# Sixteen of 96 idle TensorE products taken out, and a new issue order for all engines

## Chip, cores and metric

The kernel runs on one core of a Trainium2 (trn2) chip. The metric is the device time of one execution in microseconds (us). Times come as the median of several executions with the lowest and highest beside it. One further execution was taken with the hardware profiler; it is called the profiled execution here, and all rows of the trace are from it.

## What is computed

Eight batches, eight heads of 64 columns, 576 positions; 32 packed queries `p` per head. First the packed queries attend to `k` and `v`, then `q` attends to the result. The eight heads side by side are a matrix `x` of 576 x 512 per batch, which goes through a gated block:

```python
p_packed = sm_attn(p, k, v)
out = sm_attn(q, p_packed, p_packed)          # sm_attn: softmax(qq kk^T / 8) vv
x = out.transpose(0, 2, 1, 3).reshape(B, S, H * D)
gate_pre += conv_w[k] * xp[:, k:k + S, :]     # k = 0..4, causal
gate = 1 / (1 + exp(-gate_pre))
val = x @ w_val
return gate * val @ w_out
```

## The kernel before

The work of a batch `b` is cut into steps, each written as a generator of the kernel function. In the names of the trace and of the order:

- `keys` (line 415) and `queries` (423): VectorE (DVE) turns the loaded `pm`, `km`, `qm` into `pT`, `kT`, `qT` by 32x32 transposes.
- `attn_pack` (426): TensorE (PE) makes the scores `s1` from `kT` and `pT`; DVE takes the maximum (`nb1`), ScalarE (ACT) the exponential into `a1`; PE transposes `a1` into `at`, ACT copies that to `a1t`, PE multiplies it with `vm` into `pv`; ACT and DVE scale this to `ppd`.
- `packed_turned` (548): PE transposes `ppd` into `ppTt`, ACT copies it to `ppT`.
- `attn_out` (557) and `weighted_group` (588): PE makes the scores `s2` from `qT` and `ppT`; DVE transposes them into `t2` and takes the maximum, GpSimd (POOL) subtracts, ACT takes the exponential; DVE sums and inverts (`rs2`), POOL multiplies, DVE transposes back into `a2`, ACT rounds it to `a2h`, POOL keeps the rest as `a2l`.
- `packed_values` (610): PE makes `wp` from `ppT` and the weights `wv`; ACT and DVE split it into `wph` and `wpl`.
- `mixed` (625) and `convolved` (654): PE makes `x`; for batches 0 and 1 the convolution is folded into that product by `kx`, a product of `ppd` and the taps `cwb`. `gate` (696): for the other batches five taps on ACT and DVE, then a tanh on ACT (`sig`).
- `value` (715): PE makes `val` in four column blocks `val_b_0` to `val_b_3` of 12 products; DVE multiplies each with the gate, ACT rounds it to `gvh`, POOL keeps the rest as `gvl`.
- `project` (761): PE multiplies `gvh` and `gvl` with `woh` and `wol` into `o`, 12 products for each 128 rows; ACT copies it to `osb`, SyncE (SP) stores it. For the last batch five accumulators are filled round by round, one round for each column block of `val`.
- `value_weights`, `conv_weights` and `out_weights` (331, 340, 367) turn the float64 weights into float32 by several steps on ACT, DVE and POOL (`from_double`, 309: `wv_top`, `wv_words`, `wo_top`, `wo_words`, `cw_top`, `cw_words`).
- `keep_busy` (534) issues products of `ident` into the unread tile `spare`, two for each token of the order. These are the idle products: their result is used by nobody.

All engines issue in program order. `ORDER` (line 58) is a list of tokens that says which generator takes its next step: `D` is `keep_busy`, `K`, `Q`, `V`, `P`, `L` are the loads, `W`, `C`, `O` the weights, `k`, `q`, `a`, `p`, `s`, `t`, `u`, `w`, `x`, `v`, `o` the steps above with the batch behind the letter, `g` a gate; `.n` repeats. The row of tokens thus sets the order on each engine and on SP's queue of loads. A load of `km`, `qm`, `vm` or weights waits until the one five loads before it has landed (`AT_ONCE`, lines 48 and 240). The large PSUM buffers for `s1`, `s2`, `at`, `pv`, `wp`, `x`, `val` are three (`PSB`), so PE also waits until ACT or DVE have read a buffer out. Every instruction that a generator issues is recorded under line 93, so rows are told apart by their tiles.

```python
for _ in range(BUSY):
    for _ in range(2):
        pe.matmul(
            spare.rearrange("a (n x) -> a n x", n=2),
            x[:, :P],
            x.unsqueeze(1).broadcast_to([P, 2, 2 * P]),
            start=True,
            stop=True,
        )
    yield
```

Of the kernel before, what the change touches and what calls it, by code (L numbers as in the profile page):

```python
# [57 lines left out]
ORDER = """
K0 L0.2 D0.2 W0.4 D0.2 P0.2 W0.2 L0 k0 W0.3 D0.2 W0.4 D0 k0 D0.2 K0 D0.2 W0.3 D0.2 Q0 D0 k0 L0.3 D0 V0.2 D0.2 W0.2 
D0 W0 D0.4 C0 D0.2 a0.5 C0 W0.2 q0 D0 W0 C0 k1 D0.2 O0 a0.2 Q0 D0.4 O0 a0.3 W0 C0 W0 C0 W0 O0 W0 D0.2 K1.2 O0 a0.2   # L60
O0 q0 a0.2 O0 a0.2 p0 C0.2 O0 k1 D0 k1 p0 P2.2 s0 L0 W0 s0.2 D0 O0.2 s0.3 a1.3 s0 C0 a1 D0 W0 D0 C0 s0 D0 t0.2 C0 
a1 s0 w0.2 a1.3 D0 C0 u0.2 x0 V1 D0.2 V1 a1 w0 K2 O0 u0 O0 a1 t0 O0 a1 O0.2 a1.4 O0 t0 k2.2 K2 Q1 x0 Q1 k2 a1 x0 
p1.2 u0 q1.2 V2 u0 t0 O0 x0.4 D0 a2.2 D0 a2 O0.2 a2 x1 D0 a2 K3 k3.2 K3 Q2 v0.2 | v0 k3 s1.2 v0 s1.2 v0.3 s1.2 v0.3 
V2 s1.2 a2 t1 a2.2 a3 a2 L0 O0.3 a2 s1 t1 a3.2 L0 a3 a2.2 O0 a2 P4 a3 O0 u1 Q2 a3 a2.2 O0 u1 O0.2 v0 D0 a2 D0 t1 
P4 v0 O0 v0.2 a3.3 D0 u1 w1 v0.2 V3.2 q2 p2 w1 a3.3 w1 k4 q2 a3.3 t1 p2 K4 k4 u1 a3 x1.3 p3 t1 O0 K4 O0 Q3 u1 s2 
k4 V4 s2 O0 D0 s2.5 x1.3 O0 s2 Q3 q3 O0 V4 O0.2 v1.2 x2 O0.2 K5 p3 q3 v1.2 s2 a4.3 v1 t2 a4.2 k5 Q4 v1 o0 u2 K5 t2 
o0 a4 t2 a4 k5 a4 v1 u2 t2 u2 s3 Q4 v1.2 s3 v1.2 s3.3 P6 s3 V6 o0.2 q4 x2 o0 u2 o0 v1 x2.2 q4 s3 t2 v1.2 u2 v1 s3 
w2.2 x2.2 g8 g9 o0 a4 o0 a4.4 t3 v1 o1 x2 g10 P6 k5 a4.2 w2 a5 s3 g8 Q5 o1 K6 g8 g9 V5 g8 g9.2 a4 o0 p4 g10 p4 g8 
g10 g9.2 a5.4 o0 g10.3 Q5 t3 u3.2 s4.3 o0 v2 g11 u3 t3 a5 o1 a5.2 t3 o1 s4 g11.3 g8 v2 o1.2 v2.2 g11 s4.3 v2 s4 
u3.2 o1.2 x3.3 v2 x3 s4 k6 v2.3 q5.2 x3.2 v2 o0 w3 x3 K6 t3 v2.3 g15 t4 u4 g14 w3 k6 a5 t4 o1.2 k6 V5 a5 u4 g12 a5   # L70
g11 w3 o1 v2.3 g12 u4 a5.4 t4.2 a5 g14 o2.2 g15.2 o2 a6 g14 g12 t4 g13 a6 p5.2 o2 a6.2 g14 a6 g13.2 g12 o2 g13 
g12.2 g13 g15 v3.2 o1.2 s5 g14 s5 o1 s5 u4 v3.2 K7 v3 g14 s5 g13 s5 v3 a6 g15 s5.2 o2.2 u4 x4 v3 x4.4 s5 x4 g17 x4 
o2 v3 Q6 v3 q6 g17 v3 g15 v3 g17 s5 V6 v3.3 o2 v3.2 a6 t5 u5 g16 o3 g16 a6 w4 o3 a6 g16 a6.2 g19 g17 g19 a6 u5 
w4.2 a6 g19 g16.2 t5 o3.3 g16 u5 v4.2 g18 V7.2 a6 o2 g17.2 a6 g18.2 g19 g18 o3 o2 a6 u5 g18 t5 g18 t5 g19.2 u5 
v4.3 o1 o3 x5.4 v4.2 o3 K7 Q6 k7.3 v4.2 q6 v4 x5.2 p6 x5 t5 p6 g23.3 o3.2 g23 v4 g20.2 o3.2 s6.3 v4.4 s6.2 g22 
s6.2 t6 v4 o3.2 g23.2 o2 a7 t6 a7 Q7.2 g20 a7 g21 a7.2 g22 q7.2 a7 w5 o4 a7 o4.3 s6 g22 s6 g21 a7 g20 a7.2 o4 a7 
w5 u6 w5 a7 o4.2 u6 t6 g21 a7.4 g20 p7.2 t6 g20 g21.2 v5.3 t6 s7.3 v5 g21 o4 s7.3 v5.2 g22 o3 g22 v5 g22 o4 v5.2 
x6 o4 u6 x6 v5 u6.2 s7 v5.2 x6 v5.2 x6 s7 x6 o4 v5.2 o5 x6 g24.2 o4 g24.2 x6 g24 g25 o5 w6.3 g27.2 s7 g27 g26 o5 
g26 g24 g25 g26 g25 g26 g27 o5.2 v6 o5 v6 o5.2 g26 g27 g25.2 v6 o5 x7 g26 v6.2 o5 t7.2 g27 g25 o5 u7 v6.2 u7 t7.2 
v6.8 o5.2 t7 u7 x7 o5 x7 o5 x7 v6 x7.2 g29.3 x7 g28.3 o6.2 w7.3 u7.2 g28 o6.4 g28 g29 v7 g29 g28 g30.2 o6 g29 o6   # L80
v7.3 g30 g31 v7 g31 g30 o6 v7 o6.3 g30 v7.3 g31.2 g30 g31.2 v7.7 o7.19 
"""


# [771 lines left out]
```

## Time and profile before

| | us |
|---|---|
| median of 3 executions | 275.85 (274.7 to 277.2) |
| profiled execution, own time | 275.32 |
| its span, first to last instruction | 273.3 |
| PE busy | 262.6 (96% of the span) |
| DVE busy | 229.1 (84%) |
| ACT busy | 167.0 (61%) |
| POOL busy | 133.6 (49%) |

A row of the trace gives a start and a duration in us from the start of the span. The idle time of an engine stands in brackets with the one that ended it. PE's products overlap: the duration of one is longer than the distance to the next, so the distance is taken from a group of them. A busy PE is one on which no gap between products shows. The PE clock of a row is the share of 2.4 GHz that was granted; 0.50 is 1.2 GHz.

### The profile page before, as it was taken

The numbers are of one execution on the slowest core, as the hardware profiler recorded it, in microseconds if no ns is written. First come the engines' busy times: TensorE is split into PE (matmuls) and PEld (weight loads), VectorE is DVE, ScalarE is ACT, GpSimd is POOL, SyncE is SP. The second block draws the span as 40 slices with busy tenths as digits, with TensorE's granted clock in tenths as the row PEclk, the third lists the DMA queues.
The fourth block names the chain that finished last, engine by engine and source line by source line (L and its number), as shares of the span: only waits on it lengthen the run. The fifth ranks groups of instructions, "written<-read, shape, count | busy, mean of one in ns | idle before, by whom it ended". The sixth has DMA issues, their size and how long they took to land.

```text
span 273.3 us, 8380 instructions
## 1 busy us (share of the span) xinstructions
PE 262.6 (96%) x3547; PEld 191.9 (70%) x3547; DVE 229.1 (84%) x333; ACT 167.0 (61%) x311; POOL 133.6 (49%) x130
## 2 busy tenths in 40 slices
...
GB/s 232 314 340 309 328 304 138 315 278 282 307 166 274 141 180 251 4 194 97 44 245 90 41 143 294 45 165 111 119 7 36 77 60 57 41 77 38 38 2 192
DMA packets 25731, 43.56 MB, mean 159 GB/s; under 512 B 6730, under 2 KB 6750, under 8 KB 25694
## 3 DMA queue, kind: packets, MB, share of 16 engines
...
## 4 chain that ended last, share of the span: by engine, by line
PE 84%; DMA 6%; DVE 5%; ACT 2%; issue 2%; SPq 1%; DVEq 0%; ACTq 0%
PE o L93 37%; PE val L93 19%; PE s L93 9%; PE x L93 6%; PE pv L93 4%; DMA km<-in_k_dram 3%; PE wp L93 3%; PE at L93 2%; PE spare L93 2%; DMA wv_words<-in_moe_w_val_dram 2%; DVE qT L93 1%; PE ppTt L93 1%; DMA vm<-in_v_dram 1%; DVE kT L93 1%; SPq L93 1%
## 5 line engine op out<-in xcount | busy, mean ns | idle before, releaser
L93 DVE SCALAR_TENSOR_TENSOR sig<-xp,cw,sig 128x576 f32<-128x576 f32 x96 | 77.9, 846 | 10.1 <-ACT sig L93 9.1
L93 POOL TENSOR_TENSOR gvl<-sig,gvh 128x576 fp32r<-128x576 f32 x32 | 46.1, 1444 | 36.5 <-ACT gvh L93 28.5
L93 PE MATMUL o<-woh,gvh 128*128 128x512 f32 x144 | 58.4, 406 | 0.0
L93 PE MATMUL o<-wol,gvh 128*128 128x512 f32 x144 | 56.6, 393 | 0.0
L93 PE MATMUL o<-woh,gvl 128*128 128x512 f32 x144 | 56.4, 392 | 0.0
L93 PE MATMUL val<-a2h,wph 128*128 128x288 f32 x128 | 39.7, 310 | 0.0
L93 ACT ACTIVATE osb<-o 128x512 f32<-128x512 f32 (+1 forms) x34 | 20.0, 589 | 29.0 <-PE o L93 23.7
L93 PE MATMUL val<-a2l,wph 128*128 128x288 f32 x128 | 37.7, 294 | 0.0
L93 PE MATMUL val<-a2h,wpl 128*128 128x288 f32 x128 | 37.6, 294 | 0.0
L93 POOL TENSOR_TENSOR a2l<-a,a2h 128x576 fp32r<-128x576 f32 x16 | 22.7, 1424 | 23.3 <-ACT a2h L93 14.8
L93 PEld LDWEIGHTS o<-woh,gvh 128*128 128x128 f32 x144 | 27.0, 188 | 9.5 <-ACT osb L93 2.2
L93 PEld LDWEIGHTS o<-woh,gvl 128*128 128x128 f32 x144 | 27.1, 188 | 6.7 <-POOL gvl L93 0.4
L93 ACT CAST gvh<-sig 128x576 fp32r<-128x576 f32 x32 | 21.6, 674 | 15.7 <-DVE sig L93 15.4
L93 PEld LDWEIGHTS o<-wol,gvh 128*128 128x128 f32 x144 | 27.1, 188 | 4.6
L93 POOL TENSOR_TENSOR t<-t,rs 128x576 f32<-128x576 f32 x16 | 18.4, 1161 | 23.0 <-DVE sig L93 16.9
L93 PEld LDWEIGHTS val<-a2h,wph 128*128 128x128 f32 x128 | 24.0, 188 | 7.4 <-issue 2.7
L93 DVE SCALAR_TENSOR_TENSOR sig<-sig,val 128x576 f32<-128x576 f32 x32 | 23.6, 740 | 3.9 <-PE val L93 3.7
L93 PE MATMUL spare<-ident 128*128 128x512 bf16 x96 | 24.9, 404 | 1.4 <-POOL ident masks.py:199 1.4
L93 PEld LDWEIGHTS val<-a2h,wpl 128*128 128x128 f32 x128 | 24.1, 188 | 0.5
L93 PEld LDWEIGHTS val<-a2l,wph 128*128 128x128 f32 x128 | 24.0, 188 | 0.0
L93 ACT ACTIVATE sig<-sig 128x576 f32<-128x576 f32 x24 | 16.3, 684 | 11.7 <-DVE sig L93 11.6
L93 POOL TENSOR_TENSOR t<-t,mx 128x576 f32<-128x576 f32 x16 | 18.5, 1158 | 8.9 <-DVE mx L93 5.7
...
## 6 DMA issues: line engine op xcount, KB each, us to landing
...
```

The source lines that it names most:

```text
L93: made = getattr(self.engine, op)(*args, **kw)
```

## The change

`BUSY` goes from 48 to 40 tokens, so 80 idle products are issued, not 96, and `ORDER` is another row of tokens for the same steps. Nothing else differs: the same products, transposes and copies are issued on each engine apart from the 16.

```diff
-BUSY = 48
+BUSY = 40
 ORDER = """
-K0 L0.2 D0.2 W0.4 D0.2 P0.2 W0.2 L0 k0 W0.3 D0.2 W0.4 D0 k0 D0.2 K0 D0.2 W0.3 D0.2 Q0 D0 k0 L0.3 D0 V0.2 D0.2 W0.2 
...
+D0 L0 W0.2 L0 W0.5 D0.5 W0.2 D0 K0 P0 K0 P0 k0 D0 W0 D0.6 L0 D0 L0 W0 D0 W0 D0 k0.2 D0 W0 D0 W0.2 D0 a0 W0 Q0 W0.2 
...
```

On PE the idle products stand, before: 48 at the start, then behind the steps `s1_0` 6, `at_0` 8, `pv_0` 4, `ppTt_0` 2, `s2_0` 2, `cwps` 6, `at_1` 6, `x_0_1` 2, `s1_2` 4, `pv_2` 4, `at_3` 2, `s2_2` 2. Now: 40 at the start, then behind `s1_0` 8, `at_0` 4, `pv_0` 6, `ppTt_0` 6, `cwps` 2, `wp_0` 8, `at_1` 2, `s1_2` 2, `s2_2` 2. Behind `pv_2` and `at_3` none are left. `spread`, which stood ahead of `wp_0` and `at_1`, now stands behind both. The steps that follow keep nearly the same sequence on PE; at the end `val_7_3` now stands behind the first two rounds of the last batch's `o`, where it stood ahead of the first.

SP's queue, the first loads of the program. Before:

```order
L93 DMA km_0_0_82<-in_k_dram 128x576 x2
L93 DMA wv0_words_85<-in_moe_w_val_dram 128x512 x2
L93 DMA wv1_words_88<-in_moe_w_val_dram 128x512 x2
L93 DMA p_0_105<-in_p_dram 32x8x64 x4
L93 DMA wv2_words_113<-in_moe_w_val_dram 128x512 x2
L93 DMA km_0_1_138<-in_k_dram 128x576 x2
```

Now:

```order
L93 DMA wv0_words_85<-in_moe_w_val_dram 128x512 x2
L93 DMA wv1_words_91<-in_moe_w_val_dram 128x512 x2
L93 DMA km_0_0_114<-in_k_dram 128x576 x2
L93 DMA p_0_117<-in_p_dram 32x8x64 x4
L93 DMA km_0_1_122<-in_k_dram 128x576 x2
L93 DMA wv2_words_143<-in_moe_w_val_dram 128x512 x2
```

The first half of `km_0` moved behind two weight loads, the second half moved ahead of the third weight load; ahead of `p_0` stand the same loads as before.

ACT, from the exponentials of batch 0 (`a1_0`) to the copy of its transposed products (`a1t_0`). Before:

```order
L93 ACTIVATE a1_0_199,sums_77<-s1_0_1_202,nb1_0_1_238 128x2x9x32
L93 ACTIVATE cw_words_163<-cw_words_163 20x128
L93 ACTIVATE wv3_top_248<-wv3_words_160 128x512
L93 ACTIVATE wo0_top_257<-wo0_words_165 128x512
L93 ACTIVATE wo0_words_165<-wo0_words_165 128x512
L93 COPY a1t_0_261<-at_0_262 128x1024
```

Now:

```order
L93 ACTIVATE a1_0_171,sums_77<-s1_0_1_174,nb1_0_1_225 128x2x9x32
L93 ACTIVATE cw_words_227<-cw_words_227 20x128
L93 ACTIVATE wo0_top_240<-wo0_words_229 128x512
L93 COPY a1t_0_244<-at_0_245 128x1024
L93 COPY a1t_0_244<-at9_0_246 128x128
L93 ACTIVATE wv3_top_310<-wv3_words_148 128x512
```

Two weight steps moved behind the copy.

DVE, from the second key transpose of batch 2 to the first maximum of its scores (`nb1_2_0`). Before:

```order
L93 STREAM_TRANSPOSE kT_2_1_657<-km_2_1_602 128x1152
L93 STREAM_TRANSPOSE qT_1_0_670<-qm_1_0_605 128x1152
L93 STREAM_TRANSPOSE qT_1_1_672<-qm_1_1_654 128x1152
L93 TENSOR_REDUCE nb1_2_0_766<-s1_2_0_732 128x1
L93 TENSOR_REDUCE nb1_2_1_773<-s1_2_1_733 128x1
```

Now:

```order
L93 STREAM_TRANSPOSE kT_2_1_706<-km_2_1_636 128x1152
L93 TENSOR_SCALAR wo1_words_465<-wo1_words_465 128x512
L93 SCALAR_TENSOR_TENSOR wo1_top_704<-wo1_top_704,wo1_words_465 128x512
L93 TENSOR_SCALAR wo1_words_465<-wo1_top_704 128x512
L93 STREAM_TRANSPOSE qT_1_1_756<-qm_1_1_644 128x1152
L93 TENSOR_REDUCE nb1_2_0_759<-s1_2_0_717 128x1
```

The three weight steps of `wo1`, which stood some six instructions earlier, now stand between the transposes; `qT_1_0` moved ahead of this stretch.

## Rows read from the trace of the kernel before

**Rows 1.** The page: engines' shares of the span; of the chain that ended last.

```profile
PE 262.6 (96%) x3547; PEld 191.9 (70%) x3547; DVE 229.1 (84%) x333; ACT 167.0 (61%) x311; POOL 133.6 (49%) x130
...
PE 84%; DMA 6%; DVE 5%; ACT 2%; issue 2%; SPq 1%; DVEq 0%; ACTq 0%
```

**Rows 2.** Windows: stretch, us; busy (instructions) PE, PEld, DVE, ACT, POOL; PE clock, DMA share, GB/s.

```profile
26.41:49.30 22.89, 22.70 (x488) 13.63 (x489) 20.00 (x30) 14.03 (x31) 16.53 (x14) 1.00 0.81 260
49.30:74.60 25.30, 24.04 (x513) 18.23 (x512) 23.23 (x40) 17.94 (x40) 18.96 (x17) 1.00 0.91 293
74.60:150.00 75.40, 75.22 (x1154) 56.67 (x1156) 73.43 (x105) 49.54 (x93) 39.76 (x38) 1.00 0.49 155
150.00:255.00 105.00, 104.13 (x1133) 81.62 (x1122) 91.09 (x121) 68.99 (x117) 45.94 (x45) 1.00 0.26 88
```

**Rows 3.** Timeline of PE, opening: start, us, what, count [idle before, who ended it].

```profile
1.38 12.47 PE L93 MATMUL spare<-ident 128*128 128x512 bf16 x48 [1.38 <-POOL ident masks.py:199]
14.25 0.72 PE L93 MATMUL s<-kT,pT 32*32 32x288 f32 x16 [0.40 <-DVE kT L93]
15.51 1.47 PE L93 MATMUL s<-kT,pT 32*32 32x288 f32 x48 [0.54 <-DVE kT L93]
16.91 1.47 PE L93 MATMUL spare<-ident 128*128 128x512 bf16 x6
19.38 1.20 PE L93 MATMUL at<-ident,a 128*128 128x128 f32 x9 [1.00 <-ACT a L93]
```

**Rows 4.** The tile spare: duration of one product, ns min/median/max.

```profile
L93 PE MATMUL spare<-ident x96: 379/379/634, 1.4 to 74.8; 128*128 128x512 bf16 x96
```

**Rows 5.** Timeline of the opening, ACT and DVE.

```profile
10.03 0.63 ACT L93 ACTIVATE p<-p 128x512 f32<-128x512 f32 x1 [2.24 <-DMA p<-in_p_dram]
...
10.70 0.45 DVE L93 STREAM_TRANSPOSE pT<-p 128x256 f32<-128x256 f32 x1 [1.83 <-ACT p L93]
...
12.82 2.63 DVE L93 STREAM_TRANSPOSE kT<-km 128x1152 f32<-128x1152 f32 x2
```

**Rows 6.** Timeline of ACT, the steps ahead of the copies a1t of batches 0 and 1.

```profile
19.61 0.68 ACT L93 ACTIVATE wv_top<-wv_words 128x512 f32<-128x512 f32 x1
...
21.34 1.16 ACT L93 COPY a1t<-at 128x1024 f32<-128x1024 f32 x2
...
37.45 0.70 ACT L93 COPY cwb<-spread 128x640 f32<-128x640 f32 x1
38.04 0.28 ACT L93 COPY a1t<-at 128x128 f32<-128x128 f32 x1
```

**Rows 7.** Timeline of DVE, its two longest waits between 30 and 80 us.

```profile
48.71 1.42 DVE L93 TENSOR_REDUCE nb<-s 128x1 f32<-128x576 f32 x2 [1.20 <-PE s L93]
...
74.61 0.79 DVE L93 STREAM_TRANSPOSE t<-s 128x576 f32<-128x576 f32 x1 [1.29 <-PE s L93]
```

**Rows 8.** PE's longest wait after 26 us, and the chain's piece ahead of it.

```profile
68.68 1.26 DVE qT L93
...
72.42 0.55 PE L93 MATMUL ppTt<-ident,ppd 128*128 128x128 f32 x3 [1.26 <-ACT ppd L93]
```

**Rows 9.** Windows behind PE's last product (columns as in rows 2).

```profile
267.00:269.40 2.40, 2.30 (x9) 1.57 (x9) 1.37 (x2) 0.61 (x2) 0.00 (x0) 1.00 0.59 219
...
271.40:271.60 0.20, 0.00 (x0) 0.00 (x0) 0.00 (x0) 0.00 (x0) 0.00 (x0) 0.95 1.03 389
271.60:271.80 0.20, 0.00 (x0) 0.00 (x0) 0.00 (x0) 0.00 (x0) 0.00 (x0) 0.50 0.90 338
```

**Rows 10.** The end: the chain's run of o, and the steps behind val (busy, mean ns).

```profile
255.30 11.65 PE o L93 x51
...
L93 POOL TENSOR_TENSOR gvl<-sig,gvh 128x576 fp32r<-128x576 f32 x32 | 46.1, 1444 | 36.5 <-ACT gvh L93 28.5
...
L93 ACT CAST gvh<-sig 128x576 fp32r<-128x576 f32 x32 | 21.6, 674 | 15.7 <-DVE sig L93 15.4
...
L93 DVE SCALAR_TENSOR_TENSOR sig<-sig,val 128x576 f32<-128x576 f32 x32 | 23.6, 740 | 3.9 <-PE val L93 3.7
```

More of the change, by code (lines that the diff above doesn't have):

```diff
@@ L58 @@
 ORDER = """
-K0 L0.2 D0.2 W0.4 D0.2 P0.2 W0.2 L0 k0 W0.3 D0.2 W0.4 D0 k0 D0.2 K0 D0.2 W0.3 D0.2 Q0 D0 k0 L0.3 D0 V0.2 D0.2 W0.2
[L60 to L78, printed above, removed]
@@ L79 @@
-g26 g24 g25 g26 g25 g26 g27 o5.2 v6 o5 v6 o5.2 g26 g27 g25.2 v6 o5 x7 g26 v6.2 o5 t7.2 g27 g25 o5 u7 v6.2 u7 t7.2
-v6.8 o5.2 t7 u7 x7 o5 x7 o5 x7 v6 x7.2 g29.3 x7 g28.3 o6.2 w7.3 u7.2 g28 o6.4 g28 g29 v7 g29 g28 g30.2 o6 g29 o6
-v7.3 g30 g31 v7 g31 g30 o6 v7 o6.3 g30 v7.3 g31.2 g30 g31.2 v7.7 o7.19
+D0 L0 W0.2 L0 W0.5 D0.5 W0.2 D0 K0 P0 K0 P0 k0 D0 W0 D0.6 L0 D0 L0 W0 D0 W0 D0 k0.2 D0 W0 D0 W0.2 D0 a0 W0 Q0 W0.2
+D0.3 W0.3 a0.3 L0.2 C0 a0 q0 D0 C0 O0 a0.4 V0.2 D0.2 a0.2 Q0 W0 k1 W0 O0.2 K1.2 C0 D0.2 a0 O0 C0 O0 C0.3 W0.3 a0.2
@@ new lines @@
+O0 D0 a0.2 q0 k1.2 V1 p0 D0.3 O0 p0 W0 s0 W0 O0.2 s0 C0 s0.4 Q1 D0 a1.2 s0 a1.3 L0 w0 C0 D0.2 s0 t0.2 a1 D0.2 s0
+a1 V1 D0 u0 t0 u0 w0.2 u0 C0 a1 C0 a1 x0 P2.2 q1 a1.2 u0 t0 a1.3 x0 K2.2 k2 a1.2 Q1 x0 p1 x0.2 k2 t0 p1 x1 O0 k2
+O0.2 x0.2 O0 a2 O0 V2 O0 q1 O0 a2 K3.2 a2 D0 u0 v0 a2 k3.2 v0 a2.2 | v0 O0 s1.2 a2.2 k3 s1 a2 O0 v0 V2 L0 O0 s1.3 v0
+Q2.2 v0.2 O0 P4 s1.2 v0 s1 v0.4 t1 a3.4 q2 a3 O0 a2.2 O0 V3.2 a2.3 P4 O0 t1 a2 v0.2 a3.2 a2 a3.2 w1 O0 w1 p2 u1.2
+t1 O0.3 w1 u1 a3.2 q2 p2 a3.2 t1 a3 K4.2 v0.2 a3.2 x1 L0 x1.2 t1 p3 u1.2 k4.2 s2 p3 k4 s2 O0 s2 O0 s2.2 D0 s2.2
```

16 lines of the change are left out of this document (added).

## The prediction

> **What bounds the kernel now.** I read the page's shares first. PE is busy for 96% of the span and carries 84% of the chain that ended last; DVE is busy for 84% [rows 1]. Such shares mix stages, so the windows come next, one for each stage [rows 2]. From 26.41 us on the reader is to see two engines close to full at once. Between 49.30 and 74.60 PE is idle for 25.30 - 24.04 = 1.26 us and DVE for 25.30 - 23.23 = 2.07 us. Between 74.60 and 150 PE is idle for 0.18 us and DVE for 1.97 of 75.40 us. Only after 150 does DVE have room (13.91 us idle of 105) while PE still has almost none (0.87). So up to 150 us the end of PE's row of products and the end of DVE's row of transposes, reductions and gate steps are nearly the same thing, and an idle product that is taken from PE gains time only as far as DVE comes earlier too.
>
> Third, the timeline of PE in the opening [rows 3]: 48 idle products fill 12.47 us, then PE waits for `kT` of DVE (0.40 and 0.54 us), later for the exponential `a` (1.00 us). The opening is set by loads, DVE and ACT; the idle products there cost nothing. Fourth, the waits after it: one large one on PE, 1.26 us ahead of `ppTt` at 72.42, at the end of a chain through DVE's `qT` and ACT's `ppd` [rows 8], and two on DVE, 1.20 us for `s1_2` and 1.29 us for `s2_2` [rows 7].
>
> **The change part by part.** The sum is made against the profiled execution's own time, 275.32 us: a span of 273.3 and 2.0 around it. That is 0.5 under the median of 275.85 and inside the range of the three runs.
>
> *Price of an idle product.* The six behind the first scores take 1.47 us, the last of them 0.38 [rows 3, 4], so they stand (1.47 - 0.38) / 5 = 0.22 us apart. Sixteen are worth 3.5 us of PE at most. Eight of them are in the first block.
>
> *Opening, to the first scores.* Eight products fewer, 8 x 0.22 = 1.8 us. PE then waits for `kT` longer: 0.40 + 1.8 = 2.2 us. For `kT` to come earlier, `p` must land earlier: DVE stood idle for 1.83 us until ACT had scaled `p`, which itself waited 2.24 us for the load [rows 5]. Ahead of `p` in the new queue stand the same loads, `km_0_0`, `wv0` and `wv1`, in another order. Behind `pT` DVE has the same work up to the end of `kT` (12.82 + 2.63 = 15.45). `wv0` and `wv1` do arrive earlier, but ACT and DVE only wait less often before `p`. I take 0. Bounds: 0.5 either way, about the 0.40 and 0.54 that PE waits for the two halves of `kT`.
>
> *From there to the first `val`, at 49.3.* PE has 38 idle products where it had 40: -0.4 us. The copy `a1t_0` can start up to one ACTIVATE of 0.68 us earlier, since `wv3_top` now stands behind it [rows 6], but behind `ppTt_0` there are now six products where there were two, 4 x 0.22 = 0.9 us, and that takes it back. `spread` now runs behind `at_1`, and ACT's queue still has `cwb` ahead of the last piece of `a1t_1` (0.70 and 0.28 us) [rows 6], so `pv_1` starts later, by some 0.6 us. Four products fewer between `x_0_1` and `val_0_0` gives 0.9 back. On DVE the three steps of `wo1` now stand ahead of `qT_1_1` and `nb1_2`; they wait for ACT's `wo1_top`, which stands behind gate steps that wait for PE's `x_0_0`. Behind them on DVE wait `nb1_2` and everything that frees the PSUM buffers for `s2_1`. The cover is the 1.20 us that DVE idles at this place now [rows 7]. -0.4 - 0.7 + 0.9 + 0.6 - 0.9 = -0.5, of which DVE's part leaves me -0.3. Bounds: -1.1 (the two products and the ACTIVATE, nothing given back) to +1.2 (the idle time of DVE used up and as much again lost).
>
> *49.3 to 74.6.* Two idle products stand where eight stood: 6 x 0.22 = 1.3 us off PE, and with the wait of 1.26 at 72.42 at most 2.6. But this wait shows that PE was early: the chain came through `qT` (1.26 us) on DVE and `ppd` on ACT [rows 8]. The new order has the transposes of `q` and the steps of `wo2` at other places, with the same amount of DVE work. DVE cannot save more than its 2.07 us of idle time, 1.29 of which is one wait for PE's `s2_2` that moves with PE [rows 2, 7]. I take -0.6, nearer to what DVE's short waits leave (2.07 - 1.29 = 0.78) than to PE's 2.6. Bounds: -2.1 and 0.
>
> *74.6 to 255.* No idle product stands here in either order. PE's idle time is 0.18 + 0.87 = 1.05 us [rows 2], and no permutation of the same products can gain more than that apart from the seams between blocks. I take -0.4. Bounds: -1.05, and +1.3 for one new wait as long as the one at 72.42.
>
> *The end.* `val_7_3` moves behind two rounds of `o`. Its `gvl` is needed one round and the nine products of `o_7_8` later: 21 products, 11.65 / 51 = 0.23 apart, 4.8 us. It takes 0.74 + 0.67 + 1.44 = 2.85 us on DVE, ACT and POOL [rows 10]. Covered with 1.9 us to spare, so 0. If that cover is gone because DVE comes late, up to +0.7.
>
> Sum: 0 - 0.3 - 0.6 - 0.4 + 0 = -1.3 us, and 275.3 - 1.3 = 274.0. All lower bounds together give 275.3 - 4.75 = 270.6, all upper ones 275.3 + 3.7 = 279.0.
>
> *A rule to weigh: the clock in the opening.* Idle products also keep PE from standing still. The granted clock reads 1.00 (2.4 GHz) through the waits of 0.40, 0.54 and 1.00 us that the opening has now; by these rows a wait costs only itself. Behind the last product, which ends before 269.40, it still reads 0.95 in 271.40 to 271.60 and 0.50 (1.2 GHz) from there on [rows 9]: some 2.2 us without a product were followed by the lower level. The new wait of 2.2 us is as long. The Trainium skill, TensorE: Matmul & The Clock Gate, section What's actually happening, says that the slow level is the default and that activity releases it. The trace agrees as far as it goes: the longest idle product takes 634 ns against a median of 379 [rows 4]. By that rule a fall would not end by itself, and the second rival's time would hold.
>
> **Rivals.** *PE alone sets the time.* Then DVE's row closes up with PE's: the eight products behind the first scores are gained in full (1.8), the wait at 72.42 goes (1.26), and 0.4 comes after that: 275.3 - 3.5 = 271.8. For it: PE's 84% of the chain [rows 1], and that DVE's two longest waits are for PE [rows 7]. Against it: DVE is full for 73.43 of 75.40 us right behind the place [rows 2].
>
> *The clock falls in the opening wait.* Place: the 2.2 us ahead of the first scores. Price: a start at the slow level can be read from the first block. 48 products at 0.22 would take 47 x 0.22 + 0.38 = 10.7 us, and they took 12.47 [rows 3], so 1.8 us went. If instead everything that PE does up to the first `at` runs at half speed, it is 0.72 + 1.47 + 1.47 = 3.7 us more. The middle is 2.7, and these are now scores on the chain, with no filler behind which it could hide but the 1.00 us ahead of `at`. Together with the other terms: 275.3 - 1.3 + 2.7 = 276.7, slower than before. It decides from the point where its price passes 1.3 us. For it: the fall at the end of the run [rows 9]. Against it: at the end nothing at all follows, while here scores come in between, and no wait of up to 1.00 us did it.
>
> **How the numbers follow.** A measurement of this kernel can tell about 1%, 2.75 us, from no change. The forecast, DVE letting through a part, from 272.6 to 275.6: 0.48. PE alone, 270.6 to 273: 0.32. The fall of the clock, 275.6 to 278.5: 0.14. Something else, a new wait after 74.6 above all: 0.06. The range that leaves out 2 in 10 is 270.7 to 277.6; the forecast's own is 272.6 to 275.6. Faster by over 1% (under 272.6): most of the second case and a little of the first, 0.36. Slower by over 1% (over 278.1): a third of the clock case, most of the unnamed one and some of the forecast's own error, 0.13. Within: 0.51.
>
> **What would show it.** Right: `kT` of batch 0 ends at about 15.4; PE idles for about 2.2 us ahead of the first scores with the clock at 1.00; `val_0_0` starts within 1 us of 49.3; the wait ahead of `ppTt_3` is still there or has become several smaller ones for DVE between 49 and 75; PE's idle time after the opening is larger than now by 1 to 2 us, and DVE's row is as full. Wrong: the block at 49 to 75 shorter by over 2 us, or `kT` earlier than 14.5 (then PE alone); scores of batch 0 that take twice as long, with a granted clock of 0.50 (then the clock); a wait of over 1 us on PE after 75.

## The result, and the profile after

Over 19 executions of each, the changed kernel has a median of 278.05 us (276.92 to 279.87) against 276.66 (274.70 to 278.59): a ratio of 1.0052, 95% interval 1.0028 to 1.0076, about 1.4 us slower. Ten further executions beside another set of runs gave 1.0036 (1.0004 to 1.0068). I had forecast 1.3 us less. Ratios here and below are worked out from the single executions and leave out those over 1.5% above the fastest of their kernel, so they can differ from the ratio of two medians by some tenths of a per cent.

The profiled execution took 279.05 us with a span of 277.1. That is 1.0 above the median of its kernel, while the 275.32 from which I predicted proved to be 1.3 below its own. So the two traces lie 3.7 us apart where the medians lie 1.4 apart, and part of the difference below is scatter.

The page after: engines' shares, the chain's shares, and the queue that brings the engines' code.

```profile
PE 264.1 (95%) x3531; PEld 190.3 (69%) x3531; DVE 230.5 (83%) x333; ACT 166.1 (60%) x311; POOL 133.8 (48%) x130
...
q8 instruction: 27, 0.44, 0.7%
...
PE 80%; DVE 6%; DMA 5%; issue 4%; ACT 2%; POOL 1%; ACTq 0%; POOLq 0%; DVEq 0%
```

Sixteen products are gone and PE is busy 1.5 us longer than in [rows 1]. Its share of the chain fell from 84% to 80%, "issue" (the engine waits for nothing that the profile shows) rose from 2% to 4%. Next the opening, PE's timeline, to be laid beside [rows 3]:

```profile
1.38 11.46 PE L93 MATMUL spare<-ident 128*128 128x512 bf16 x40 [1.38 <-POOL ident masks.py:199]
15.71 0.72 PE L93 MATMUL s<-kT,pT 32*32 32x288 f32 x16 [2.87 <-DVE kT L93]
16.97 2.44 PE L93 MATMUL s<-kT,pT 32*32 32x288 f32 x48 [0.54 <-DVE kT L93]
19.35 2.42 PE L93 MATMUL spare<-ident 128*128 128x512 bf16 x8
22.02 1.20 PE L93 MATMUL at<-ident,a 128*128 128x128 f32 x9 [0.25 <-ACT a L93]
```

Two things are to be seen. PE waits 2.87 us where I had 2.2, and the 48 score products behind the wait take 2.44 us where they took 1.47. The windows of that stretch (columns as in rows 2) say why the second:

```profile
15.00:17.00 2.00, 0.74 (x20) 0.21 (x20) 2.00 (x3) 0.68 (x2) 1.85 (x2) 1.00 0.88 307
17.00:18.00 1.00, 1.00 (x33) 0.51 (x34) 0.90 (x2) 0.00 (x0) 0.00 (x0) 0.51 1.06 317
18.00:19.00 1.00, 1.00 (x32) 0.36 (x15) 0.46 (x2) 0.00 (x0) 0.38 (x1) 0.50 0.97 332
19.00:20.00 1.00, 1.00 (x10) 0.28 (x3) 0.58 (x1) 0.00 (x0) 0.92 (x2) 0.50 1.07 396
20.00:21.00 1.00, 1.00 (x5) 0.39 (x4) 1.00 (x3) 0.79 (x3) 1.00 (x1) 0.78 0.87 253
21.00:22.00 1.00, 0.77 (x4) 0.15 (x2) 1.00 (x1) 1.00 (x5) 0.04 (x1) 1.00 0.96 295
```

The granted clock fell to 0.50 (1.2 GHz) behind the wait and came back during 20 to 21 us, while PE worked without a gap. And the wait is longer because `kT` starts 1.47 us later than in [rows 5]. The timeline of ACT and DVE:

```profile
11.77 0.63 ACT L93 ACTIVATE p<-p 128x512 f32<-128x512 f32 x1 [2.95 <-DMA p<-in_p_dram]
...
12.43 0.45 DVE L93 STREAM_TRANSPOSE pT<-p 128x256 f32<-128x256 f32 x1 [5.54 <-ACT p L93]
...
14.29 2.63 DVE L93 STREAM_TRANSPOSE kT<-km 128x1152 f32<-128x1152 f32 x2
```

`p` landed 1.74 us later, although its loads were issued earlier (the first at 3.80 us instead of 4.01): from issue to landing took 6.4 to 6.9 us where it had been 4.5 to 4.7. And DVE stood idle for 5.54 us instead of 1.83: with the weights ahead in the queue its weight steps were done before, and nothing was left to do.

| start of | before | after | later by |
|---|---|---|---|
| first scores of batch 0 | 14.25 | 15.71 | 1.5 |
| `at_0` | 19.38 | 22.02 | 2.6 |
| `val_0_0` | 49.32 | 51.95 | 2.6 |
| scores `s2_2` | 72.89 | 74.52 | 1.6 |
| `val_1_0` | 78.05 | 81.00 | 2.9 |
| scores `s1_7` | 185.69 | 188.15 | 2.5 |
| last product's end | 269.30 | 273.05 | 3.7 |

So the opening loses 2.6 us, the stretch from `val_0_0` to `s2_2` gains 1.0 back, and what stands right behind loses 1.3: the scores `s2_2` 0.27 and the product `x_1_1` 1.05, of which the stop below is 0.36. Another 1.2 us are lost between 188 us and the end. PE's timeline of the kernel before there, in which `x_1_1` is one row of 80 products:

```profile
72.89 1.71 PE L93 MATMUL s<-qT,ppT 32*32 32x288 f32 x64
...
75.07 3.05 PE L93 MATMUL x<-a,kx 32*64 32x288 f32 x80
```

And of the changed kernel:

```profile
74.04 0.55 PE L93 MATMUL ppTt<-ident,ppd 128*128 128x128 f32 x3
74.52 1.98 PE L93 MATMUL s<-qT,ppT 32*32 32x288 f32 x64
...
76.97 2.06 PE L93 MATMUL x<-a,kx 32*64 32x288 f32 x42
79.39 1.68 PE L93 MATMUL x<-a,kx 32*64 32x288 f32 x38 [0.36 <-issue]
...
199.79 0.32 PE L93 MATMUL pv<-vm,a1t 64*32 64x64 f32 x8 [0.83 <-issue]
...
220.66 0.50 PE L93 MATMUL o<-woh,gvh 128*128 128x512 f32 x1 [0.69 <-ACT osb L93]
```

The wait of 1.26 ahead of `ppTt_3` [rows 8] is gone; a shorter one of 0.48 stands at 68.35 us, ahead of another `ppTt`. New are two stops inside a run of equal products with nothing to wait for that the profile shows (0.36, 0.83), and one for ACT's `osb` (0.69; the kernel before has none there, but one of 0.55 for ACT's `xp` at 235.64 us). Last the windows of the two stages up to `x_1_1` that answer to the first two of [rows 2] (the second ends at the start of `x_1_1`, half a microsecond further on in the work than there), and behind them DVE's two waits that answer to the first of [rows 7].

```profile
28.24:51.95 23.71, 23.12 (x486) 13.29 (x487) 20.94 (x31) 13.89 (x31) 15.90 (x14) 1.00 0.85 256
51.95:76.97 25.02, 24.37 (x508) 17.63 (x506) 23.93 (x41) 17.92 (x41) 18.83 (x17) 1.00 0.86 268
```

DVE's timeline:

```profile
48.23 0.44 DVE L93 TENSOR_SCALAR wo_words<-wo_words 128x512 uint32<-128x512 uint32 x1 [1.13 <-ACT wo_top L93]
...
51.77 1.42 DVE L93 TENSOR_REDUCE nb<-s 128x1 f32<-128x576 f32 x2 [0.62 <-PE s L93]
```

Between 51.95 and 76.97 DVE is now idle for 25.02 - 23.93 = 1.09 us where it had 2.07: it closed up, as forecast.

### The profile page after: what moved, and what is told of

Same layout as the page of the kernel before. It is cut to its first block, busy times and chain, and to the rows that moved or that the text cites. A ratio compares the mean times of both kernels' runs of the same rounds, so it can differ in the third digit from the quotient of the medians.

```text
span 277.1 us, 8347 instructions
## 1 busy us (share of the span) xinstructions
PE 264.1 (95%) x3531; PEld 190.3 (69%) x3531; DVE 230.5 (83%) x333; ACT 166.1 (60%) x311; POOL 133.8 (48%) x130
## 4 chain that ended last, share of the span: by engine, by line
PE 80%; DVE 6%; DMA 5%; issue 4%; ACT 2%; POOL 1%; ACTq 0%; POOLq 0%; DVEq 0%
PE o L93 37%; PE val L93 17%; PE s L93 9%; PE x L93 8%; PE pv L93 3%; DMA km<-in_k_dram 2%; DMA wv_words<-in_moe_w_val_dram 2%; PE wp L93 2%; PE at L93 1%; PE ppTt L93 1%; DVE nb L93 1%; PE spare L93 1%; DVE kT L93 1%; DVE mx L93 1%; DVE rs L93 1%
## 5 line engine op out<-in xcount | busy, mean ns | idle before, releaser
L93 DVE SCALAR_TENSOR_TENSOR sig<-xp,cw,sig 128x576 f32<-128x576 f32 x96 | 78.9, 850 | 12.3 <-ACT sig L93 11.2
L93 POOL TENSOR_TENSOR gvl<-sig,gvh 128x576 fp32r<-128x576 f32 x32 | 45.5, 1425 | 55.1 <-DVE sig L93 27.2
L93 PE MATMUL o<-woh,gvh 128*128 128x512 f32 x144 | 59.0, 410 | 0.7 <-ACT osb L93 0.7
L93 PE MATMUL val<-a2h,wph 128*128 128x288 f32 x128 | 39.1, 305 | 0.0
L93 POOL TENSOR_TENSOR t<-t,rs 128x576 f32<-128x576 f32 x16 | 19.1, 1196 | 20.4 <-DVE sig L93 12.1
L93 PE MATMUL spare<-ident 128*128 128x512 bf16 x80 | 22.1, 427 | 1.4 <-POOL ident masks.py:199 1.4
```

The lines of the kernel that those rows point to most:

```text
L93: made = getattr(self.engine, op)(*args, **kw)
```

## Experiments

The theories at this point: the *clock* (the wait lets it fall), the *loads* (their new order brings `p` late), *new waits* behind 75 us, and that the late idle products save little because DVE sets that stretch. In all runs the kernel before was timed on the same chip; ratios are to it, 1% being 2.77 us.

**The opening, on the new order.** Four kernels differ in the order of the first loads and in the idle products that stand ahead of the first scores. Twelve products more (e1_fill_wait; e7_new_loads_fill8 has `D0.5` and 44, eight more):

```diff
-BUSY = 40
+BUSY = 46
-D0 L0 W0.2 L0 W0.5 D0.5 W0.2 D0 K0 P0 K0 P0 k0 D0 W0 D0.6 L0 D0 L0 W0 D0 W0 D0 k0.2 D0 W0 D0 W0.2 D0 a0 W0 Q0 W0.2 
+D0 L0 W0.2 L0 W0.5 D0.5 W0.2 D0 K0 P0 K0 P0 k0 D0 W0 D0.6 L0 D0 L0 W0 D0 W0 D0 k0.2 D0 W0 D0 W0.2 D0.7 a0 W0 Q0 W0.2 
```

The old order of the first loads (e2_old_loads; e3_old_loads_fill adds the eight products of e7 to it):

```diff
-D0 L0 W0.2 L0 W0.5 D0.5 W0.2 D0 K0 P0 K0 P0 k0 D0 W0 D0.6 L0 D0 L0 W0 D0 W0 D0 k0.2 D0 W0 D0 W0.2 D0 a0 W0 Q0 W0.2 
+K0 D0 L0 W0.2 L0 W0.5 D0.5 W0.2 D0 P0 L0 K0 P0 k0 D0 W0 D0.6 D0 L0 W0 D0 W0 D0 k0.2 D0 W0 D0 W0.2 D0 a0 W0 Q0 W0.2 
```

> The changed kernel with twelve idle products more, placed right ahead of the first scores, so that its wait of 2.87 us there shrinks to 2.87 - 12 x 0.22 = 0.2 us; everything else is as changed. Clock theory (the wait let the granted clock fall to 0.50 and the slow scores behind it cost time to the end): the granted clock stays at 1.00 between 15 and 21 us, the second half of s1_0 takes about 1.5 us as before the change and not 2.44, val_0_0 starts 1 to 1.5 us earlier than 51.95, and the time is 0.9 to 1.5 us under the changed kernel, at or just under the kernel before (ratio 0.998 to 1.002). Load theory (p comes late because of the order of the loads, the clock is a side show): kT still ends at 16.9, val_0_0 moves by under 0.5 us, the ratio stays at 1.004 to 1.006. Theory of new waits behind 75 us: the opening gets shorter, but the time does not follow, ratio 1.003 to 1.006.

> The changed kernel with the first loads in the order of the kernel before (km_0_0 first, then wv0, wv1, p_0, wv2, km_0_1), still 40 idle products at the start. Load theory: p lands 1 to 1.7 us earlier, kT of batch 0 starts at about 12.9 instead of 14.29, PE's wait ahead of the first scores falls from 2.87 to about 2.2 us or less, and val_0_0 comes about 1 us earlier; the time 0.7 to 1.4 us under the changed kernel (ratio 1.000 to 1.003), and if the clock still falls in the shorter wait, only half of that. If p's landing varies with the chip and not with the queue: no earlier kT, ratio 1.004 to 1.006. Clock theory alone: the clock still falls in a wait of 1.4 to 2.2 us and the ratio stays within 1.002 to 1.006.

> Both at once: the changed kernel with the old order of the first loads and eight idle products more ahead of the first scores, so 48 stand there as in the kernel before. If the opening is all that the change lost: s1_0, at_0 and pv_0 start as in the kernel before or up to 0.8 us earlier, val_0_0 at 48.5 to 49.5, and the time is 0.5 to 1.5 us under the kernel before (ratio 0.994 to 0.998). If new waits behind 75 us hold the end: val_0_0 within 0.5 us of 49.3, but ratio 1.000 to 1.004.

> The changed kernel with eight idle products more ahead of the first scores; against the run with the old order of the loads and the same eight products it differs in the loads' order alone. Load theory: that run was at 0.9996 of the kernel before, this one is 0.7 to 2 us slower, ratio 1.002 to 1.007, with a wider scatter of single times. If the loads' order does nothing: ratio 0.998 to 1.002, and the 1.0047 of the run with twelve products was scatter or came from its four products more.

> The changed kernel once more, beside the others on one chip. Clock theory: the granted clock falls again behind the wait ahead of the first scores (mean clock 0.993 or 0.994 in nearly all executions). Load theory: kT of batch 0 starts at 13.5 or later again. Stalls of PE by its own code: PE stands still again with 'issue' at the same products of its stream, the 1237th, 2130th or 3024th, and not at others. Ratio 1.003 to 1.008 by all of them.

| loads | products ahead of the first scores | ratio (95%) |
|---|---|---|
| old | 48 | 0.9996 (0.9968 to 1.0023); again 0.9999 (0.9970 to 1.0028) |
| old | 40 | 1.0018 (0.9990 to 1.0045) |
| new | 48 | 1.0023 (0.9988 to 1.0058) |
| new | 52 | 1.0047 (1.0006 to 1.0088) |
| new | 40: the changed kernel | 1.0052 (1.0028 to 1.0076); again 1.0036 (1.0004 to 1.0068) |

With both parts of the opening undone the changed kernel equals the kernel before, so the loss lies in the opening. One part alone is worth some 0.5 to 0.6 us, both together 1.0 to 1.4; but the intervals of the single parts reach 1, that of the changed kernel does not, so how the loss is shared out is not settled. In the repeated profile of the changed kernel `p` was late again (11.60 us), PE waited 2.92, the second scores took 2.46 us, and PE stopped at the same products. In the run with the old loads and 40 products the wait was 1.54 us in the profile, the clock stayed (mean 0.998), and the scores took 1.47; over its executions, though, the mean clock was below 0.995 in 7 of 12. The run with 52 products is a miss: the wait was gone, the clock at 1.00 and `val_0_0` 2.2 us earlier in its profile, as the clock theory had it, yet its time did not fall. Its single times scatter from 275.80 to 281.35, with a median of 279.13; I can't say why.

**The opening, on the old order.** The same two edits on the kernel before: eight of the 48 products out (e4_before_less8, with 44 tokens), and the new order of the loads (e5_before_new_loads).

```diff
-D0 W0 D0.4 C0 D0.2 a0.5 C0 W0.2 q0 D0 W0 C0 k1 D0.2 O0 a0.2 Q0 D0.4 O0 a0.3 W0 C0 W0 C0 W0 O0 W0 D0.2 K1.2 O0 a0.2 
+D0 W0 C0 D0.2 a0.5 C0 W0.2 q0 D0 W0 C0 k1 D0.2 O0 a0.2 Q0 D0.4 O0 a0.3 W0 C0 W0 C0 W0 O0 W0 D0.2 K1.2 O0 a0.2 
```

```diff
-K0 L0.2 D0.2 W0.4 D0.2 P0.2 W0.2 L0 k0 W0.3 D0.2 W0.4 D0 k0 D0.2 K0 D0.2 W0.3 D0.2 Q0 D0 k0 L0.3 D0 V0.2 D0.2 W0.2 
+L0.2 K0 D0.2 W0.4 D0.2 P0.2 K0 W0.2 L0 k0 W0.3 D0.2 W0.4 D0 k0 D0.4 W0.3 D0.2 L0 Q0 D0 k0 L0.2 D0 V0.2 D0.2 W0.2 
```

> The kernel before with eight of its 48 idle products ahead of the first scores taken out and nothing else changed. Clock theory: PE waits 0.40 + 1.8 = 2.2 us ahead of the first scores, the granted clock falls to 0.50 behind that wait, the scores of batch 0 take up to twice as long, and the time is 0.7 to 1.5 us over the kernel before (ratio 1.002 to 1.006). My prediction's own step (the wait costs only itself and the products cost nothing there): the clock stays at 1.00 and the ratio is 0.999 to 1.001.

> The kernel before with only the first loads in the order of the changed kernel (wv0, wv1, km_0_0, p_0, km_0_1, wv2, wv3, qm_0_0); 96 idle products and every other instruction at its old place. Load theory: p lands 0.5 to 1.7 us later than in the kernel before in most executions, kT of batch 0 starts at 13.3 to 14.3 instead of 12.82, PE waits 0.9 to 1.9 us ahead of the first scores, and the ratio to the kernel before is 1.002 to 1.006. If the loads' order is without effect and p's landing only scatters: ratio 0.998 to 1.002. Clock theory: the granted clock falls in some of the executions, where the wait passes some 2 us, and stays in the others.

Eight products fewer: 1.0032 (1.0003 to 1.0061). PE's timeline and two windows of that run:

```profile
1.38 10.98 PE L93 MATMUL spare<-ident 128*128 128x512 bf16 x40 [1.38 <-POOL ident masks.py:199]
14.82 0.72 PE L93 MATMUL s<-kT,pT 32*32 32x288 f32 x16 [2.47 <-DVE kT L93]
16.08 2.45 PE L93 MATMUL s<-kT,pT 32*32 32x288 f32 x48 [0.54 <-DVE kT L93]
...
16.00:17.00 1.00, 0.92 (x32) 0.46 (x33) 0.90 (x3) 0.00 (x0) 0.04 (x1) 0.52 0.96 324
17.00:18.00 1.00, 1.00 (x32) 0.45 (x15) 0.56 (x2) 0.32 (x1) 0.27 (x1) 0.50 1.01 381
```

Nothing but the eight products was changed, and the clock fell here too. The first scores start 0.57 us later than in [rows 3] (`p` landed that much later in this execution), `at_0` 1.56 later, `val_0_0` 1.46, and no step after it makes that good. The clock's price up to `at_0` is thus 1.56 - 0.57 = 1.0 us in this profile. Profiles with a fall in the opening have a mean clock of 0.992 or 0.993, those without one 0.996 or more (the two with two loads at once, further down, apart). Over the executions it was below 0.995 in 9 of 12 of this run, in 18 of 19 of the changed kernel, in 7 of 10 when that was repeated, and in 4 of 157 of the kernel before. What such a fall costs at the end is not shown by them: the nine executions of this run have a mean of 277.74 us, the three others 277.56.

The new loads on the old order: 1.0031 (0.9991 to 1.0070), `kT` at 13.58 instead of 12.82, the clock at 1.00. Over all profiles `p` can be scaled at 9.65 to 11.53 us (mean of 14: 10.44) with the old order of the loads and at 10.74 to 11.77 (mean of 5: 11.21) with the new one. So the order of the loads is worth some 0.8 us of `p`, and half of what the two single profiles differ by was scatter. What it is worth in time this run alone does not show, as its interval reaches 1.

**The late idle products.** First the last sixteen taken out of the kernel before (e6_before_less16_late; the last eight tokens `D` of the order, 48 products stay at the start). Three of the five lines that change:

```diff
-BUSY = 48
+BUSY = 40
-p1.2 u0 q1.2 V2 u0 t0 O0 x0.4 D0 a2.2 D0 a2 O0.2 a2 x1 D0 a2 K3 k3.2 K3 Q2 v0.2 | v0 k3 s1.2 v0 s1.2 v0.3 s1.2 v0.3 
+p1.2 u0 q1.2 V2 u0 t0 O0 x0.4 a2.2 a2 O0.2 a2 x1 a2 K3 k3.2 K3 Q2 v0.2 | v0 k3 s1.2 v0 s1.2 v0.3 s1.2 v0.3 
...
-V2 s1.2 a2 t1 a2.2 a3 a2 L0 O0.3 a2 s1 t1 a3.2 L0 a3 a2.2 O0 a2 P4 a3 O0 u1 Q2 a3 a2.2 O0 u1 O0.2 v0 D0 a2 D0 t1 
+V2 s1.2 a2 t1 a2.2 a3 a2 L0 O0.3 a2 s1 t1 a3.2 L0 a3 a2.2 O0 a2 P4 a3 O0 u1 Q2 a3 a2.2 O0 u1 O0.2 v0 a2 t1 
...
-k4 V4 s2 O0 D0 s2.5 x1.3 O0 s2 Q3 q3 O0 V4 O0.2 v1.2 x2 O0.2 K5 p3 q3 v1.2 s2 a4.3 v1 t2 a4.2 k5 Q4 v1 o0 u2 K5 t2 
+k4 V4 s2 O0 s2.5 x1.3 O0 s2 Q3 q3 O0 V4 O0.2 v1.2 x2 O0.2 K5 p3 q3 v1.2 s2 a4.3 v1 t2 a4.2 k5 Q4 v1 o0 u2 K5 t2 
```

Then the same with small products at the start, so that PE's program is as long as before (e8_late16_as_small: 44 of the usual size and 20 small ones), and the kernel before with ten of its 48 made small (e9_less8_with_small: 38 and 10, `range(19, 24)`). In `keep_busy`, and for the first also `D0.12` in place of `D0.4`:

```diff
-        for _ in range(BUSY):
+        for i in range(BUSY):
...
+                if i in range(20, 30):
+                    pe.matmul(spare[:, :32], x[:, :P], x[:, :32], start=True, stop=True)
+                    continue
```

> The kernel before without its last sixteen idle products (two of the six behind at_1 and all behind x_0_1, s1_2, pv_2, at_3 and s2_2); the 48 at the start stay. If PE alone sets the time from 36 to 75 us: up to 16 x 0.22 = 3.5 us less, ratio 0.987 to 0.993. If DVE lets through a part, as I forecast: 0.3 to 1.5 us less, ratio 0.995 to 0.999. If nothing of it comes through (DVE's row holds, or the time goes into new waits of PE behind 75 us, at the places where PE stood with 'issue' in the changed kernel): ratio 0.999 to 1.002.

> The kernel before without its last sixteen idle products, and with twenty small ones (32 columns each) in the place of four of the 48 at the start, so that PE's program holds as many products ahead of every later step as the kernel before. Code theory (the sixteen gained nothing because PE's own code then arrives late: its ninth block of code was fetched during the wait ahead of ppTt_3 in the kernel before, where PE stood at its 1142nd product, but not where that wait stood at the 1128th or 1134th): here the wait stands at 1142 again, the ninth packet of the instruction queue starts inside it, there is no 'issue' gap near the 1237th product, x_1_1 takes 3.0 us up to val_1_0 instead of 4.42, and the ratio is 0.995 to 0.999, against 1.0014 without the small products. If DVE's row or something else holds the time: x_1_1 is short but the time stays, ratio 0.999 to 1.002. If the place of the code is not it: the gap near the 1237th product is there again.

> The kernel before with ten of its 48 idle products at the start replaced by ten small ones of 32 columns: PE's program stays as long, but PE waits some 2 us ahead of the first scores. Clock theory: the granted clock falls behind that wait in most executions, the ratio is 1.001 to 1.005, below the 1.0032 of the run that took eight out by the part that its code lost (about 0.3 us in its profile near the 1237th product). If all that the eight cost came from the code's place: ratio 0.998 to 1.001 although the clock falls. Code theory: no 'issue' gap at the 1237th product, the ninth packet of the instruction queue starts while PE stands at the 1142nd.

Without the 16: 1.0014 (0.9983 to 1.0044). With small ones in their place: 1.0036 (0.9999 to 1.0073). Neither saves time, so PE alone does not set it there; that rival had 0.987 to 0.993. Ten of the 48 made small: 1.0001 (0.9972 to 1.0029), with a wait of 1.55 us and the clock at 1.00 in its profile. Over its executions the mean clock was below 0.995 in 5 of 12, and these are no longer than the others (means of 276.66 and 276.64 us). This leaves a rival for the 1.0032 of the run with eight products out: that run also shortened PE's program by eight products, this one did not. No run parts the two, and the waits were not equal. In the other runs that have both kinds of executions those with the low clock are longer by 0.6 us (old loads with 40 products), 0.7 (the changed kernel, repeated) and 2.1 (the late 16 as small ones); a late `p` would lengthen both the wait and the time, so this is no price of the clock either.

PE's timeline of the second around `x_1_1`:

```profile
72.25 0.55 PE L93 MATMUL ppTt<-ident,ppd 128*128 128x128 f32 x3 [0.71 <-ACT ppd L93]
72.72 1.71 PE L93 MATMUL s<-qT,ppT 32*32 32x288 f32 x64
74.36 0.70 PE L93 MATMUL x<-a,kx 32*64 32x288 f32 x4
75.27 1.19 PE L93 MATMUL x<-a,kx 32*64 32x288 f32 x21 [0.21 <-DVE t L93]
77.94 2.17 PE L93 MATMUL x<-a,kx 32*64 32x288 f32 x55 [1.48 <-issue]
```

And of the third:

```profile
72.57 0.55 PE L93 MATMUL ppTt<-ident,ppd 128*128 128x128 f32 x3 [0.98 <-ACT ppd L93]
73.05 1.70 PE L93 MATMUL s<-qT,ppT 32*32 32x288 f32 x64
...
75.22 1.56 PE L93 MATMUL x<-a,kx 32*64 32x288 f32 x25
78.01 0.74 PE L93 MATMUL x<-a,kx 32*64 32x288 f32 x16 [1.23 <-issue]
```

Without the 16, `x_1_1` starts 0.71 us earlier than in the kernel before (74.36 against 75.07): DVE let through 0.7 of 3.5 (in the profile without small products, counted from the first scores, 0.3). But PE then stops for 1.48 us and goes on at 77.94, at the same time as the other run (78.01), which came 0.86 later to the place. The gain is waited away. The third run shows the size of the scatter: it keeps within 0.17 us of the kernel before from `at_0` to `x_1_1`, loses 1.9 us there, and is 1.99 behind at the end.

My theory on this stop, that PE's code was fetched early in the kernel before because PE's wait ahead of `ppTt_3` stood at its 1142nd product, fell: here it stands at the 1144th and the 1142nd again, and the stops were 1.48 us, the longest of all, and 1.23.

What the stop waits for can be read from the traces, though no run moved it alone. Queue 8 brings instructions in packets of 16 KB, and their number goes with the length of PE's program: 27 in the four profiles with 3531 products, 28 in the fifteen with more. I take them for PE's code. e3_old_loads_fill has one in the window from 74.8 to 75.8 us, by the DMA view:

```profile
q8 instruction: 1, 0.02, 5.5%
```

and PE's timeline of that run reads

```profile
71.47 0.55 PE L93 MATMUL ppTt<-ident,ppd 128*128 128x128 f32 x3
71.95 1.95 PE L93 MATMUL s<-qT,ppT 32*32 32x288 f32 x64
...
74.36 1.66 PE L93 MATMUL x<-a,kx 32*64 32x288 f32 x34
77.30 1.71 PE L93 MATMUL x<-a,kx 32*64 32x288 f32 x46 [1.27 <-issue]
```

In every profile the place is the 1236th or 1237th product recorded on PE, however many idle ones stand ahead, so it is a place in the program's length, not in the work. The ninth packet of the queue in some of the traces:

| kernel | packet starts, us | PE is at product | PE goes on, us | later by | stop |
|---|---|---|---|---|---|
| before | 71.49 | 1142 | | | none |
| new loads on the old order | 73.20 | 1142 | | | none |
| after | 77.14 | 1197 | 79.39 | 2.25 | 0.36 |
| after, again | 76.58 | 1197 | 79.06 | 2.48 | 0.63 |
| less 8 | 75.89 | 1201 | 78.25 | 2.36 | 0.13 |
| old loads | 74.82 | 1213 | 77.14 | 2.31 | 1.02 |
| old loads, 48 | 74.86 | 1213 | 77.30 | 2.44 | 1.27 |
| late 16 as small | 75.66 | 1231 | 77.94 | 2.29 | 1.48 |
| less 10, small ones | 75.80 | 1223 | 78.01 | 2.21 | 1.23 |

In all twelve profiles with a stop here, PE goes on 2.2 to 2.5 us after the packet started; where the packet came some 95 products or more ahead (five profiles) there was none, and in two it came at the 1201st without an idle stop. Seven and fourteen packets further, at the 2130th and 3024th product, the same stops come in some profiles (0.99 us at 130 us in e1_fill_wait, 0.83 at 198.96 in the changed kernel).

**Fewer loads under way.** Does the burst of loads hold the packet back? In the loads' `fetch`, here with the numbers of e14_combined_four_late; e12 and e13 have 58 and 3, e10 and e11 have 28 and 2. The runs named before are the kernel before, those named combined are e3_old_loads_fill with the edit.

```diff
-        if len(under_way) >= AT_ONCE:
+        at_once = AT_ONCE if len(under_way) < 58 else 4
+        if len(under_way) >= at_once:
...
-                under_way[-AT_ONCE],
+                under_way[-at_once],
```

> The kernel before, in which from the 29th load on (vm_3_0, issued at about 57 us) at most two loads are under way at once instead of five; order and products as before. If the ninth packet of PE's code waits behind the burst of loads between 57 and 77 us: it starts within 1.5 us of PE's stop at the 1142nd product in every execution, no 'issue' gap at the 1237th product, and as the kernel before has that gap in part of its executions only, the median falls by 0.5 to 1.2 us (ratio 0.995 to 0.998). If the loads do not hold it: packet at 75 to 76 us as in the two runs with small products, ratio 0.999 to 1.002. If two at once are too few: DVE waits for km or qm, ratio over 1.003.

> The changed kernel with the old order of the first loads, eight idle products more ahead of the first scores, and at most two loads under way from the 29th on. Without the last edit it came to 0.9996 of the kernel before, with a gap of 1.27 us at the 1237th product. If the loads hold PE's code: the packet starts ahead of 74 us, the gap is under 0.4 us, and the ratio is 0.993 to 0.997, faster than both kernels. If they do not: the gap stays, ratio 0.999 to 1.001. If two at once are too few: waits for loads between 75 and 110 us, ratio over 1.002.

> The kernel before with at most three loads under way instead of five, but only from the second half of vm_3_0 on (the burst of 57 to 77 us and what follows). If this burst holds back the ninth packet of PE's code: it starts before PE's 1190th product, the stop at the 1237th is gone or under 0.3 us, and the median falls by 0.3 to 1 us (ratio 0.996 to 0.999). If it does not hold it: packet at the 1197th to 1231st product, ratio 0.999 to 1.002. If three are too few for the loads: DVE or PE waits for km, qm or vm between 75 and 125 us, ratio over 1.003.

> The same edit on the changed kernel with the old order of the first loads and eight idle products more ahead of the first scores (0.9996 of the kernel before, with a stop of 1.27 us at the 1237th product). If the burst holds the code: packet before the 1190th product, stop under 0.4 us, val_1_0 at 77.0 to 78.0 instead of 78.94, ratio 0.994 to 0.998. If not: stop of 0.4 to 1.3 us as before, ratio 0.999 to 1.001.

> As the last, with four loads under way instead of three: by the theory that the burst holds PE's code a stop between those of three and of five loads (0.2 to 0.9 us) and a ratio of 0.996 to 0.999; if three are too few for the loads, this one shows the gain without that loss. Without the theory: ratio 0.999 to 1.001.

> The changed kernel with the old order of the first loads and eight idle products more ahead of the first scores, five loads under way, once more beside the next run: ratio 0.998 to 1.001 as the first time (0.9996). Theory that PE's code comes late: a stop at the 1237th product that ends 2.2 to 2.5 us after the ninth packet of the instruction queue starts, as in the profiles so far.

> The same with at most four loads under way from the second half of vm_3_0 on, once more: if the 0.9964 of the first time was no scatter, 0.995 to 0.998 and at least 0.5 us under the run beside it; if it was, the two are equal within 0.3 us. By the theory that the burst of loads holds the code, the stop at the 1237th product is under 0.5 us.

Two at once: 1.0822 (1.0778 to 1.0866) and 1.0757 (1.0709 to 1.0805). The count goes by halves of a load, so the edit took hold far ahead of 57 us: the 29th half, issued at 25.49 us in the kernel before, went out at 30.69, and the loads came too late; PE's timeline of the first:

```profile
79.63 0.44 PE L93 MATMUL pv<-vm,a1t 64*64 64x128 f32 x4 [2.06 <-DMA vm<-in_v_dram]
82.72 1.56 PE L93 MATMUL pv<-vm,a1t 64*64 64x128 f32 x24 [2.65 <-DMA vm<-in_v_dram]
```

The packet did start early in both (at the 1118th and 1137th product) and no stop followed.

Three at once, later: on the kernel before 0.9995 (0.9966 to 1.0024), its packet at the 1142nd product and no stop, as without the edit; on the changed order with the old opening 0.9965 (0.9937 to 0.9994). Four at once on the latter: 0.9964 (0.9938 to 0.9989), and again 0.9961 (0.9940 to 0.9982) with a median of 275.62 us, beside 276.31 for the same kernel with five and 276.80 for the kernel before. So this last version is about 1 us faster than the kernel before and, by the ratios, 2 to 2.5 us faster than the changed one. Its reason isn't settled: the packet still started at the 1201st to 1203rd product, not ahead of the 1190th as expected, and the kernel with five loads had no idle stop either in its second profile. The stops here were 0.45, 0.17 and none, against 1.27 and none with five loads; at the 2130th product they were at most 0.10 us, against 0.74 and 0.38.

## Why the prediction was wrong

*The base.* I summed from 275.32 and called it 0.5 under the median of three. Against the median of 19 it is 1.3 under: that execution had PE's code in time, and the run that keeps within 0.17 us of it up to 75 us shows what goes with a late packet, 1.9 us. A sum of 1.3 us cannot rest on one execution here.

*Opening, to the first scores: the step that failed.* "Ahead of `p` in the new queue stand the same loads … I take 0.", bounds 0.5. The same loads in another order brought `p` 0.8 us later on the mean, 1.74 in the profile: by the runs some 0.6 us (new loads with 48 products) to 0.9 (on the old order), both with intervals that reach 0. With the opened wait, the opening as a whole cost 1.0 to 1.4 us where I had taken 0, and this is clear of noise. `p` was not issued later, it took longer to land; what of the queue delays it was not tried.

*The clock.* I had the mechanism as a rival with 0.14 and a price of 2.7 us. It happened: both waits that follow from taking out eight products (2.47 alone, 2.87 with late loads) were followed by a clock of 0.50. Its price up to `at_0` was 1.0 us in the profile of the run that takes out nothing else, not 2.7: only the last 48 of the 64 score products and the idle products behind them ran slowly, and the latter ran into PE's wait ahead of `at_0`, which shrank from 1.00 to 0.54 us. How much of it reaches the end the executions do not show. The sign that I had named was there, scores that take 2.44 / 1.47 = 1.7 times as long at 0.50. The Trainium skill, TensorE: Matmul & The Clock Gate, section What's actually happening, has the slow level as the default and activity as what releases it. The traces agree: the higher level came back between 20 and 21 us, PE having worked at 0.50 without a gap since 17 us. My sentence behind the rule, that a fall would not end by itself, led me astray: the slow scores and idle products were work, and the clock came back during it.

*To the first `val`.* Right in its parts: DVE waits 1.13 us for `wo1_top` and then only 0.62 for `nb1_2`. With the opening restored, `val_0_0` starts at 49.40 in e3_old_loads_fill, 0.1 later than before; but its first scores start 0.35 later too, and counted from them it is 34.80 us against 35.07, the -0.3 that I took. In the second profile of that kernel it is 35.27. In the sum, +0.9 and -0.9 count again what the net -0.4 holds; they cancel.

*49.3 to 74.6.* I took -0.6, and on the mean it came out. From `val_0_0` to `s2_2` the five profiles with the old order and all late idle products take 23.56 to 23.58 us. The ten with the new order (without the one with two loads at once) take 22.54 to 23.56, so they gain 0.0 to 1.0, on the mean 0.6. The wait ahead of `ppTt_3` went, and in the changed kernel DVE lost half its idle time.

*74.6 to 255: the second step that failed.* I took -0.4, with one new wait of up to 1.3 as the upper bound. The new wait is there, right behind the gain, and by the traces it is for PE's own code, which I had not thought of. From `s2_2` to `val_1_0` the kernel before takes 5.16 us and the same ten profiles 5.62 to 6.99. So on the mean more is lost there than was gained ahead of it: both stretches together take 29.2 us instead of 28.7. Both the new order and the mere removal of the late products come to the 1237th product sooner after `val_0_0`, while the packet starts at 74.4 to 77.1 us instead of 71.5. The timed runs say the same: all that stands behind the opening gives nothing (0.9996 and 0.9999 with the old opening), where my terms gave -1.3. That a packet in time would give the time back no run shows.

*The end.* As forecast: behind 221 us PE has no wait of over 0.12 us, so `val_7_3` was covered. The 1.2 us that the changed kernel loses behind 188 us are ahead of it: the stop of 0.83 and the wait of 0.69, less the 0.55 of before, make 1.0 of them.

By the runs the sum is thus: the opening +1.0 to +1.4, the rest of the order 0. Inside the opening the loads are about +0.6 and the wait, with its clock, about +0.5; on the changed order neither is clear of noise alone, and on the old order only the eight products are (1.0003 to 1.0061).
